# Three causal selects per head group in place of seven, with exponentials stored in another layout and other instruction orders

## The chip, the cores and the metric

The kernel runs on one core of a Trainium2 chip. The metric is the device time of one launch in microseconds. The engines named below are PE (TensorE: matmuls; its weight loads are shown apart as PEld), DVE (VectorE), ACT (ScalarE), POOL (GpSimd) and SP (SyncE, which here issues nearly all DMAs). Every engine has a queue of its own that it works off in order, and engines wait for each other through semaphores.

## The reference, cut to what matters

Two branches read the same 2048 tokens of width 640 and are mixed by a per-token gate g.

Branch A is causal attention inside four segments of 512 tokens, 32 heads of width 20, joined with a memory that is carried from segment to segment:

```
for s in range(4):
    logits = einsum('bhqd,bhkd->bhqk', qs, ks) * scale + mask
    a_dot  = softmax(logits) @ vs
    a_mem  = (phi(qs) @ M) / (phi(qs) @ z + 1e-6)
    o      = g_h * a_mem + (1 - g_h) * a_dot
    M, z   = M + phi(ks).T @ vs, z + sum(phi(ks))
a = o @ wo
out = g * a + (1 - g) * irfft2(rfft2(x) * W)
```

The mask adds -1e9 where the key's position lies behind the query's. Branch B is the filter in the frequency domain in the last line; the kernel does its transforms as matmuls with tables.

## The kernel before

**Staging.** The four segments are worked off in turn. For each one, `project` makes q, k and v, q and k go through a scratch tensor in DRAM into the padded tiles `qkp` (one head per 32 partitions), `attend` does the attention, `mem_update` and `mem_read` the memory. The transforms of branch B (`fft`) run beside segments 0 to 3. `finish_tile` does the last projection with `wo`, adds branch B and stores; for segments 0 to 2 it first needs the reciprocals of the softmax denominators, which go through DRAM: `denominators` loads them (`dnc`), inverts them (`dnr`, L1340), multiplies with a gate (`rc`, L1342), stores them (`r_scr<-rc`) and `finish_tile` loads them again spread over partitions (`r<-r_scr`); then the five steps named `normal` multiply them into `oU` (L1656).

**Attention.** A head group is four heads, so a segment has 8 groups and the kernel 32. Groups are taken in pairs, and a pair has five units (`UNITS`, L580; `qk_unit`, L1356), each of which is a bundle of small matmuls into one and the same block of four PSUM banks, followed by the exponential on ACT from PSUM into the tile `ex` (L1393). Kind 0 (unit a) takes the 512 queries against the first 64-key blocks, kind 1 (unit b) the rest, kind 2 (unit c) what is left of both groups of the pair; the order inside a pair is a, b of the first group, a of the second, c of both, b of the second. Units a and c use weights 64 columns wide, so that two keys' blocks lie beside each other in the array, and unit b uses weights 128 columns wide:

```
    PIECES = (((0, 0, 0, 0, 0, 512), (1, 64, 64, 128, 0, 64), (0, 64, 64, 64, 64, 448)),
              ((1, 0, 0, 192, 0, 320), (2, 0, 0, 320, 320, 192)),
              ((2, 0, 0, 256, 0, 64), (3, 64, 64, 384, 0, 128), (3, 0, 0, 448, 64, 64)))
```

A piece is (128-key block, first key in it, first partition of the result, first query, first column of the result, columns), and each piece is done once for each of the four heads. Segment 3 needs another layout of `ex` for its own way of multiplying with v (`pv_group` instead of `pv_flipped`), so there unit b's exponential is split in two (1280 and 768 elements a partition) and unit c's too (512 each).

**Causal selects.** Whole diagonal blocks are computed, and POOL then sets to zero what lies ahead of the query (`mask`, L1411; the instruction is at L1414). A group has seven selects: two after its exponential a, two after b, three after c; four of them cover 256 elements a partition, two cover 512 elements on 64 partitions, one 512 on 128. The product with v (`pvf` or `pv`) waits for all of them. `ex` has three buffers for the 32 groups.

**The order.** Nothing is placed at run time. `record` lists some 2,300 steps with their dependences, `ORDER` is a list written out by hand or program that says in which order and on which engine each step is issued (an even entry takes a step's first engine, an odd one its second), and `schedule` (L112) only derives the PSUM banks and waits from it. The list `ENDED` is used for one thing: where a step has several waits, `emit` (L254) issues the one first whose step stands later in `ENDED`. Steps made by `either` may go to DVE or POOL, those by `copy_alts` (evacuations of PSUM) to ACT or DVE. On PE the matmuls of one step are issued together; steps have a mode (full array, `qk` tiles of 20 x 64 or 20 x 128, 32-column tiles, 64-column tiles), and neighbours of one mode need no switch of the array.

## Time and profile before

| what | value |
|---|---|
| time, median of 3 runs | 241.98 us (241.62 to 243.56) |
| span of the profiled execution, first to last instruction | 247.9 us (the page gives no other time of it) |
| PE busy | 230.0 us, 93%, 3849 matmuls |
| PEld busy | 139.7 us, 56% |
| DVE busy | 196.3 us, 79% |
| ACT busy | 199.7 us, 81% |
| POOL busy | 165.7 us, 67% |
| selects on POOL (L1414) | 224, together 121.0 us |
| exponentials on ACT (L1393) | 92, together 138.7 us |
| mean granted TensorE clock | 0.972 of full speed |

In the rows of a profile, "out<-in" names the tiles written and read, then follow partitions and elements a partition, the count, the busy time and the mean of one. Numbers behind the last bar are the idle time that the engine had just before these instructions and what ended it. A row of the timeline has the start and the length in microseconds, the engine, the line and the operation; SPq and ACTq are instructions that issue DMAs. Three engines are busy over 79% of the span, so a wait of one of them is mostly filled by the others; the chain of work that ended last tells which one set the end.

### The profile page before, as it was taken

To read this page: it belongs to the slowest core of one execution; us is meant where nothing else is said; L and a number is where in the kernel's file an instruction comes from. 1 tells how busy PE (TensorE), PEld (TensorE's weight loads), DVE (VectorE), ACT (ScalarE), POOL (GpSimd) and SP (SyncE) were. 2 spreads that over 40 slices of the span, in tenths; PEclk is the share of its full clock that TensorE was granted. 3 is DMA by queue.
4 is the path that set the end of the run, shared out by engine and by line. 5 is a ranking of instruction groups with operands and counts; after the bars stand their busy time and mean duration, and the time that the engine had idled before them with its cause. 6 is when DMAs were issued, how large, how long until landed. Compare 5 with 4: busy or idle time off the path is not lost.

```text
span 247.9 us, 9233 instructions
## 1 busy us (share of the span) xinstructions
PE 230.0 (93%) x3849; PEld 139.7 (56%) x3849; DVE 196.3 (79%) x481; ACT 199.7 (81%) x241; POOL 165.7 (67%) x297
## 2 busy tenths in 40 slices
PE   7899999999999999998899999999999975699994
PEld 2574667765465665545566554455444543366794
DVE  0489998799999987888998979979888831755653
ACT  2289688998999989999999899999999864278740
POOL 8532278367969658478939998949898660559640
PEclk9999999999999999999999999999999995599999
DMA  7999979937875864768697543447665977382123
GB/s 174 281 361 206 229 191 230 269 91 203 222 173 163 199 213 114 206 95 252 170 242 208 165 131 99 122 146 192 188 183 128 282 101 81 35 118 81 59 81 109
DMA packets 58924, 42.11 MB, mean 170 GB/s; under 512 B 30020, under 2 KB 55172, under 8 KB 58884
## 3 DMA queue, kind: packets, MB, share of 16 engines
q1 hardware_dynamic: 57844, 40.96, 66.4%
q8 instruction: 30, 0.49, 0.8%
q10 hardware_dynamic: 1040, 0.57, 0.8%
q14 instruction: 10, 0.08, 0.2%
HBM read 23.32 MB, written 12.30 MB: 144 GB/s over the span
## 4 chain that ended last, share of the span: by engine, by line
PE 59%; DVE 15%; DMA 12%; ACT 8%; SPq 3%; issue 2%; DVEq 0%
PE psum L521 52%; PE psum L519 6%; ACT ex L1393 5%; DMA r<-r_scr 3%; DMA r_scr<-rc 3%; DVE Pt L1569 3%; DMA Wt<-in_B_w_i_dram 2%; DMA wk<-in_A_wk_dram 2%; DMA qk_scr<-qu 2%; SPq L553 2%; DVE G L1615 1%; SPq L555 1%; DVE oU L1656 1%; DVE phk L1213 1%; DVE va L1244 1%
## 5 line engine op out<-in xcount | busy, mean ns | idle before, releaser
L1393 ACT ACTIVATE ex<-psum 128x2048 bf16<-128x2048 f32 (+4 forms) x92 | 138.7, 1507 | 13.2 <-PE psum L521 11.4
L1414 POOL TENSOR_SCALAR_AFFINE_SELECT ex<-ex 128x256 bf16<-128x256 bf16 (+2 forms) x224 | 121.0, 562 | 41.2 <-ACT ex L1393 38.3
L521 PE MATMUL psum<-qkp 20*64 20x64 bf16 (+5 forms) x1024 | 31.8, 268 | 4.0 <-ACT ex L1393 2.1
L521 PE MATMUL psum<-xT,wk 128*128 128x256 bf16 (+1 forms) x280 | 33.9, 273 | 0.6 <-DMA wk<-in_A_wk_dram 0.6
L521 PE MATMUL psum<-xT,wq 128*128 128x512 bf16 (+1 forms) x135 | 30.7, 381 | 0.5 <-DMA xT<-in_A_x_dram 0.5
L521 PE MATMUL psum<-wv,xT 128*64 128x320 bf16 (+3 forms) x240 | 30.1, 303 | 0.3 <-DVE va L1244 0.3
L1569 DVE TENSOR_TENSOR Pt<-psum,Wt 128x642 bf16<-128x642 f32 x32 | 25.5, 821 | 2.6 <-PE psum L521 1.5
L521 PEld LDWEIGHTS psum<-qkp 20*64 20x64 bf16 (+1 forms) x1024 | 12.2, 101 | 22.0 <-ACT ex L1393 14.8
L521 PEld LDWEIGHTS psum<-xT,wk 128*128 128x128 bf16 (+1 forms) x280 | 19.9, 97 | 7.1 <-DMA wk<-in_A_wk_dram 1.6
L519 PE MATMUL psum<-wo,oU 128*32 128x320 bf16 x480 | 23.5, 317 | 0.2 <-DVE oU L1664 0.2
L1035 POOL TENSOR_TENSOR xsb<-xf 128x320 bf16<-128x320 bf16 (+2 forms) x12 | 9.5, 788 | 16.2 <-DVE xsb L1035 12.2
L1244 DVE TENSOR_TENSOR va<-psum,ebx 128x320 bf16<-128x320 f32 x32 | 15.2, 483 | 5.0 <-ACT gate L1242 2.9
L521 PEld LDWEIGHTS psum<-wv,xT 128*64 128x64 bf16 (+1 forms) x240 | 14.9, 105 | 7.4 <-issue 2.9
L532 DVE CAST ot<-psum 128x320 bf16<-128x320 f32 x21 | 10.1, 491 | 11.2 <-PE psum L519 8.8
L521 PE MATMUL psum<-big,Cp 128*128 128x321 bf16 (+1 forms) x96 | 18.7, 310 | 0.2 <-DVE G L1615 0.2
L521 PE MATMUL psum<-big,Ac 128*128 128x160 bf16 (+2 forms) x96 | 18.1, 257 | 0.3 <-DVE Pt L1569 0.2
L521 PE MATMUL psum<-ex,va 128*32 128x512 bf16 (+4 forms) x480 | 17.3, 275 | 0.5 <-DVE mem L1289 0.2
L521 PE MATMUL psum<-tt,Yt 128*128 128x256 bf16 (+1 forms) x96 | 16.5, 276 | 1.1 <-DVE Pt L1569 0.4
L1615 DVE TENSOR_TENSOR G<-eo,psum 128x320 bf16<-128x320 f32 x32 | 14.7, 482 | 3.5 <-PE psum L521 2.5
L1201 ACT ACTIVATE et<-qu 128x512 bf16<-128x512 bf16 x25 | 15.6, 629 | 0.2
L519 PEld LDWEIGHTS psum<-wo,oU 128*32 128x32 bf16 x480 | 12.5, 100 | 5.7 <-issue 1.1
L521 PEld LDWEIGHTS psum<-ex,va 128*32 128x32 bf16 x480 | 10.1, 96 | 9.8 <-POOL ex L1414 1.7
(99 smaller groups left out, 393.7 us busy)
## 6 DMA issues: line engine op xcount, KB each, us to landing
qkp<-qk_scr SPq DMA_DIRECT2D x28, 160.0 KB
tt<-tab_tt SPq DMA_DIRECT2D x8, 512.0 KB, 3.8
qk_scr<-qu SPq DMA_DIRECT2D x12, 256.0 KB, 2.4
u_scr<-ub SPq DMA_DIRECT2D x12, 256.0 KB, 4.4
xsb<-in_A_x_dram SPq DMA_DIRECT2D x8, 320.0 KB, 5.9
oU<-u_scr SPq DMA_DIRECT2D x15, 128.0 KB, 4.0
out_dram<-ot SPq DMA_DIRECT2D x12, 160.0 KB
Wt<-in_B_w_r_dram SPq DMA_DIRECT2D x16, 80.2 KB, 3.3
```

The lines of the kernel that those rows point to most:

```text
L519: h = e.matmul(dst, wt, r_, start=st, stop=sp_, **{**kw, "tile_position": (0, q), "skip_group_check": True})
L521: h = e.matmul(o_, l_, r_, start=st, stop=sp_, **kw)
L532: alts["dve"] = (lambda e: e.tensor_copy(dst(), src()), 67 + 1.04 * n, 68.0)
L553: return e.dma_start_transpose(d_, s_)
L555: return e.dma_start(d_, s_)
L1035: self.either(lambda e, dst=dst, src=src, d0=d0, n=n, op=op: e.tensor_tensor(xs.ap(o + dst, [D, 2], [1, n]), xf.ap(src + d0, [321, 2], [1, ...
L1201: self.one("act", lambda e: e.activation(et.ap(0, [1, L]), qsl(), ACT.Exp), L, [qb], [b("et", pi_)], late, name="phi_exp")
L1244: self.one("dve", lambda e: e.tensor_tensor(va.ap(i * H * VW + h0 * VW, [VW, nh], [1, DH]), self.ps(bank, 0, [DH, nh], [1, DH]), self.ebx. ...
L1393: self.one("act", lambda e, d=d, q=q: e.activation(self.ex.ap(*d), self.ps(bank, *q), ACT.Exp, scale=SC), n, [bank], [self.exb(s, 2 * pr + ...
L1414: self.one("pool", lambda e: e.affine_select(self.ex.ap(e0 + d0, [1280, 4], [1, n], np_=np_), self.ex.ap(e0 + s0, [1280, 4], [1, n], np_=np_),
L1569: self.one("dve", lambda e, ri=ri, Pt=Pt, Wt=Wt, wo_=wo_, bank=bank: e.tensor_tensor(Pt.ap(ri * 322, [644, 2], [1, KD]), self.ps(bank, 0, ...
L1615: self.one("dve", lambda e, q=q, n2=n2, bank=bank, eo=eo: e.tensor_tensor(self.G.ap(n2 * D + 639 * q, [1 - 2 * q, 320]), eo.ap(q, [1, 320] ...
```

## The change

- The layout of `ex` is now two blocks of 640 for each head, the same in all four segments: in each, unit a's or b's 512 columns and two strips of 64. The diagonal blocks of a group's four heads then lie at one distance from each other, eight of them.
- `PIECES` gives each unit other pieces: unit b has five pieces with weights 64 columns wide instead of two with 128, unit c four instead of three. The number of columns in each unit stays. A pair has 96 small matmuls in place of 64 (kernel: 1536 in place of 1024).
- Each unit has one exponential in every segment: 80 in place of 92. Unit c writes 64-column strips of both groups with one instruction.
- A group has three selects of 512, 1024 and 1024 elements a partition, on all 128 partitions: 96 in place of 224. The first reads what a and b wrote and writes the strips between; the second finishes these and unit c's strips; the third does the first diagonal blocks. They are recorded behind unit c for the first group of a pair and behind unit b for the second, and no select starts before the group's exponentials a and b are there.
- The product with v reads the new places (`VPIECES`: 512, 128, 256, 256, 128 columns for 512, 384, 192, 64, 128).
- `ENDED` is gone; the order of waits comes from the planner's own end times. `ORDER` is another list for the 2188 steps that are left of 2328.

```diff
-VPIECES = ((0, 0, 512, 0), (1, 512, 384, 128), (2, 896, 192, 320), (2, 1088, 64, 256), (3, 1216, 128, 384))
+VPIECES = ((0, 0, 512, 0), (1, 512, 128, 128), (1, 896, 256, 256), (2, 640, 256, 256), (3, 1152, 128, 384))
...
-              ((1, 0, 0, 192, 0, 320), (2, 0, 0, 320, 320, 192)),
-              ((2, 0, 0, 256, 0, 64), (3, 64, 64, 384, 0, 128), (3, 0, 0, 448, 64, 64)))
+              ((2, 0, 0, 256, 0, 256), (3, 64, 64, 384, 0, 64), (2, 64, 64, 320, 64, 192), (1, 0, 0, 256, 256, 256), (1, 64, 64, 256, 256, 256)),
+              ((1, 0, 0, 192, 0, 64), (1, 64, 64, 192, 0, 64), (3, 0, 0, 448, 256, 64), (3, 64, 64, 448, 256, 64)))
...
+        for i, o in enumerate(sorted(ops, key=lambda o: o.t1)):
+            o.rank = i
...
+        if kind < 2:
+            d, q, n = (e0 + 640 * kind, [1280, 4], [1, 512]), (0, [512, 4], [1, 512]), 2048
         else:
-            outs = [((e0 + sh + n_ * step, [1280, 4], [320, 2], [1, 64]), (n_ * 128, [512, 4], [64, 2], [1, 64])) for n_ in range(2)]
...
+            d, q, n = (e0 + 576, [self.exo(s, g + 1) - e0, 2], [640, 8], [1, 64]), (0, [64, 2], [256, 8], [1, 64]), 1024
+        self.one("act", lambda e: e.activation(self.ex.ap(*d), self.ps(bank, *q), ACT.Exp, scale=SC), n, [bank],
+                 [self.exb(s, 2 * pr + gp, ks) for gp in gps], prio - self.QK_LEAD, name="exp")
+        if u == 3:
+            self.mask(s, 2 * pr, prio)
+        elif u == 4:
+            self.mask(s, 2 * pr + 1, prio)
...
+        def sel(d0, s0, n, base, np_):
+            return lambda e: e.affine_select(self.ex.ap(e0 + d0, [640, 8], [1, n], np_=np_), self.ex.ap(e0 + s0, [640, 8], [1, n], np_=np_),
+                                             [[0, 8], [1, n]], ALU.is_ge, 0.0, base=base, channel_multiplier=-1)
+        x = [self.exb(s, g, k) for k in ("a0", "b0", "c0", "m0")]
+        self.one("pool", sel(512, 0, 64, 64, P), 512, x[:2], x[3:], prio, per=0.793, fix=218, name="mask_first")
+        self.one("pool", sel(512, 512, P, -64, 64), 1024, [], x[2:], prio, per=0.793, fix=218, name="mask_odd")
+        self.one("pool", sel(0, 0, P, 0, P), 1024, [], x[:2], prio, per=0.793, fix=218, name="mask_even")
```

Read against the lists of steps, the two `ORDER` lists have the units of all pairs in one and the same sequence on PE, and the products with v too. They differ in what lies between. Counted in them: switches of PE's mode, 226 before and 212 after. Engines, before and after: outputs evacuated by ACT 11 and 17 of 32 (the others by DVE), products with v evacuated by ACT 8 and 12 of 24, results of the last transform (`eo`) by ACT 10 and 7 of 16, transposes for segment 3 by ACT 4 and 2 of 5, projections by ACT 22 and 21 of 39; foldings of x on POOL 16 and 10 of 51, gate tables on POOL 2 and 4 of 4, `normal` on POOL 2 and 4 of 15. On SP, the load of `wk`'s larger part stood behind the load of an `xsb` part, the transposed loads of x, `beta` and `wk`'s smaller part; now neither `xsb` nor `beta` is ahead of it. For segment 2, eleven DMAs stood between the load of `dnc` and the store of `rc` (five of them `oU` loads just ahead of it); now seven do, in this order: one `qkp`, two `oU`, `gcc`, two `qkp`, one store of outputs. Behind that store come `oU`, `qkp`, a transposed load, `oU`, `g_scr`, `oU`, and then the load of `r`.

More of the change, by code (lines that the diff above doesn't have):

```diff
@@ L110, with schedule @@
             (0, 4): 105.0, (1, 4): 105.0, (2, 4): 105.0, (4, 0): 105.0, (4, 1): 105.0, (4, 2): 105.0}
-    def schedule(self, pools, order, ended, nsem=56):
+    def schedule(self, pools, order, nsem=56):
         ops = self.ops
-        for o in ops:
-            o.rank = len(ops)
-        for i, v in enumerate(ended):
-            ops[v].rank = i
         queue = {e: [] for e in self.eng}
@@ L1361, in qk_unit @@
         gps, kind = unit
-        width = 128 if kind == 2 else 512
         items, rb = [], []
@@ L1381, in qk_unit @@
-        if kind == 0 or (kind == 1 and s < 3):
-            outs = [((e0 + 576 * kind, [1280, 4], [1, 512]), (0, [512, 4], [1, 512]))]
-        elif kind == 1:
-            outs = [((e0 + 576, [1280, 4], [1, 320]), (0, [512, 4], [1, 320])), ((e0 + 960, [1280, 4], [1, 192]), (320, [512, 4], [1, 192]))]
-        elif s < 3:
-            outs = [((e0 + sh, [1280, 4], [step, 2], [1, 128]), (0, [512, 4], [128, 2], [1, 128]))]
-        else:
-            outs = [((e0 + sh + n_ * step, [1280, 4], [320, 2], [1, 64]), (n_ * 128, [512, 4], [64, 2], [1, 64])) for n_ in range(2)]
@@ L1409 @@
-    SH23 = (1088, 896)
-    def mask(self, s, g, np_, d0, s0, n, rk, wk, prio, base, step=64):
-        e0 = self.exo(s, g)
-        self.one("pool", lambda e: e.affine_select(
-            self.ex.ap(e0 + d0, [1280, 4], [1, n], np_=np_), self.ex.ap(e0 + s0, [1280, 4], [1, n], np_=np_),
-            [[0, 4], [step, n // 64], [1, 64]], ALU.is_ge, 0.0, base=base, channel_multiplier=-1), 4 * n, [self.exb(s, g, k) for k in rk],
-            [self.exb(s, g, k) for k in wk], prio, per=0.793, fix=218, name=f"mask{d0}" + "bc"[np_ == P])
+        ks = "abc"[kind] + "0"
```

48 lines of the change are left out of this document (12 added, 36 removed), and 307 rows, old and new, of tables (ENDED, ORDER).

## The prediction

> **What bounds the kernel now.** I first read the page: busy times, chain, costliest groups.
>
> ```profile
> span 247.9 us, 9233 instructions
> PE 230.0 (93%) x3849; PEld 139.7 (56%) x3849; DVE 196.3 (79%) x481; ACT 199.7 (81%) x241; POOL 165.7 (67%) x297
> PE 59%; DVE 15%; DMA 12%; ACT 8%; SPq 3%; issue 2%; DVEq 0%
> L1393 ACT ACTIVATE ex<-psum 128x2048 bf16<-128x2048 f32 (+4 forms) x92 | 138.7, 1507 | 13.2 <-PE psum L521 11.4
> L1414 POOL TENSOR_SCALAR_AFFINE_SELECT ex<-ex 128x256 bf16<-128x256 bf16 (+2 forms) x224 | 121.0, 562 | 41.2 <-ACT ex L1393 38.3
> ```
>
> PE sets the end: 59% of the chain. POOL isn't on it at all, and its selects waited 38.3 us for exponentials. The waits say the same from the other side:
>
> ```profile
> PEld psum L521 <- ACT ex L1393: 14.8, 47, 0.7
> PEld psum L521 <- POOL ex L1414: 1.7, 6, 0.4
> ```
>
> PE's weight loads sat 14.8 us until an exponential had freed the PSUM block, but only 1.7 us, six times, until a select. What a cheaper select can give directly is 1.7 us. The stretches (columns: length, then busy time and count of PE, PEld, DVE, ACT, POOL, clock, DMA) show who could profit:
>
> ```profile
> 100.00:125.00 25.00, 23.49 (x358) 13.22 (x358) 22.93 (x58) 23.97 (x27) 18.53 (x37) 1.00 0.71 181
> 204.00:214.70 10.70, 5.92 (x122) 3.46 (x124) 4.78 (x14) 3.72 (x5) 2.20 (x3) 0.50 0.48 61
> ```
>
> In the middle PE, DVE and ACT are all above 91%, POOL at 74%. Taking work from POOL alone shortens nothing there. From 204 to 214.7 all engines idle, and the clock is at half: a hole, whose cause is read below.
>
> **The change part by part.** *Selects.* The groups by shape:
>
> ```profile
> L1414 POOL TENSOR_SCALAR_AFFINE_SELECT ex<-ex 128x256 bf16<-128x256 bf16 x128 | 59.5, 476 | 38.7 <-ACT ex L1393 37.4
> L1414 POOL TENSOR_SCALAR_AFFINE_SELECT ex<-ex 64x512 bf16<-64x512 bf16 x64 | 42.6, 670 | 1.8 <-ACT ex L1393 0.9
> L1414 POOL TENSOR_SCALAR_AFFINE_SELECT ex<-ex 128x512 bf16<-128x512 bf16 x32 | 22.0, 690 | 0.6
> ```
>
> From 256 to 512 elements a select grows by 214 ns, so 262 ns are fixed. A 1024 select isn't in the trace: the line gives 690 + 2 x 214 = 1118 ns; it may cost up to two of 512, 1380 ns. A group paid 4 x 476 + 2 x 670 + 690 = 3934 ns and will pay 690 + 2 x 1118 = 2926 (at most 3450). Over 32 groups POOL loses 32 us (at least 15) and falls to about 133 us. Hidden behind ACT and PE as shown, I cost it at 0 to -1.7 us and take 0, since the same wait can come back, next.
>
> *The wait that is added.* Selects used to start after exponential a; now a group's first needs a and b. For a group that ends with b, the time from its last exponential to v was 670 + 476 = 1146 ns and becomes 2926; for one that ends with c, 476 + 476 + 690 or so = 1.6 us becomes 2 x 1118 = 2.2. Behind the waiting select on POOL stand the other selects, W additions (L1574) and `normal`; PE's next matmuls stand behind v. What covers it is PE work between a group's last unit and its v: counted in the order lists, at least 10 steps before (median 26.5) and at least 16 after (28.5). A step takes 230.0 / 1073 = 0.214 us on average. A group that ends with b needs 0.33 + 1.88 + 2.93 = 5.1 us, 24 steps; 5 of 32 groups have fewer than they need. Added up, they are short by 1.5 us, and 3 groups before by 1.7: the new list moved v back as far as it had to. I take 0.
>
> *Exponentials.* Segments 0 to 2 keep theirs. In segment 3 the rows are
>
> ```profile
> L1393 ACT ACTIVATE ex<-psum 128x2048 bf16<-128x2048 f32 x56 | 105.2, 1879 | 7.9 <-PE psum L521 6.7
> L1393 ACT ACTIVATE ex<-psum 128x1024 bf16<-128x1024 f32 x12 | 12.3, 1023 | 1.1 <-PE psum L521 0.8
> L1393 ACT ACTIVATE ex<-psum 128x1280 bf16<-128x1280 f32 x8 | 9.9, 1239 | 3.0 <-PE psum L521 3.0
> L1393 ACT ACTIVATE ex<-psum 128x768 bf16<-128x768 f32 x8 | 6.5, 810 | 0.3
> L1393 ACT ACTIVATE ex<-psum 128x512 bf16<-128x512 f32 x8 | 4.8, 598 | 1.1 <-PE psum L521 1.0
> ```
>
> Unit b pays 1239 + 810 - 1879 = 170 ns less, eight times; unit c 2 x 598 - 1023 = 173 less, four times: -2.05 us of ACT. The new list gives ACT more evacuations (6 of outputs, 4 of products with v, less 3 `eo`, 2 transposes, 1 projection), some 2.5 us at 0.44 to 0.6 each, so ACT stays at 200 us. Bounds 0 to -2.05; the end of segment 3 lies in the hole, so I take a quarter, -0.5. Unit c's strips of 64 might stream slower; no row shows it, nearest is the 1024 form: 0.
>
> *Matmuls.* 512 more, columns unchanged. The PE timeline has each kind with its follower:
>
> ```profile
> 100.61 0.40 PE L521 MATMUL psum<-qkp 20*128 20x320 bf16 x8
> 100.94 0.63 PE L521 MATMUL psum<-tt,Yt 128*65 128x256 bf16 x4
> ...
> 103.71 0.32 PE L521 MATMUL psum<-qkp 20*64 20x64 bf16 x24
> 103.96 1.25 PE L521 MATMUL psum<-xT,wq 128*128 128x512 bf16 x5
> 105.05 0.38 PE L521 MATMUL psum<-tt,Yt 128*65 128x256 bf16 x2
> 105.36 0.43 PE L521 MATMUL psum<-qkp 20*64 20x512 bf16 x12
> 105.72 0.39 PE L521 MATMUL psum<-xT,wq 128*128 128x512 bf16 x1
> ```
>
> Unit b with 8 matmuls holds PE 0.33 us, c with 24 0.25, a with 12 0.36: PE follows columns (512, 256, 512), hardly the count. The new b (20, weights as in a) should take between its 0.33 and a's 0.36: 32 x 0.015 = +0.5 us; c with 32 stays or gains 8 x 4 ns: 16 x 0.015 = +0.2. Together +0.6, bounds 0 to +5.3 (c's 250 / 24 = 10.4 ns for each of 512).
>
> The Trainium skill, TensorEngine Tiling, Instruction Overhead, says that each matmul has an overhead of about 60 cycles and that one column takes as long as 60. By it, in a row, 512 x 25 ns = 12.8 us would be added, an estimate from that page; the 24 matmuls in 0.25 us, 10 ns each, speak against it for tiles that work side by side.
>
> *Mode switches.* Five 512-column matmuls take 105.05 - 103.96 = 1.09 us, 0.218 each; unit a with the same columns 0.36, so entering and leaving cost 0.14, or 0.07 a switch. 226 - 212 = 14 fewer: -1.0 us (0 to -2.0).
>
> *DVE beside longer selects.* One group shows what a select does to DVE, first with its mean, then with its minimum/median/maximum in ns:
>
> ```profile
> L1213 DVE TENSOR_SCALAR phq<-qu 128x512 bf16<-128x512 bf16 x15 | 5.3, 363 | 0.0
> L1213 DVE TENSOR_SCALAR phq<-qu x15: 273/283/712, 34.7 to 157.4; 128x512 bf16<-128x512 bf16 x15
> ```
>
> The slowest is 429 ns above the median, about one 256 select: it seems to be held until POOL's instruction is over. If so, the mean hold goes with the squares of the selects' lengths: 128 x 0.476² + 64 x 0.67² + 32 x 0.69² = 73 before, 32 x (0.69² + 2 x 1.118²) = 95 after, 1.3 times. The mean is 80 ns above the median; some 130 of DVE's instructions read bf16 from SBUF alone as this one does, so they may be held 10 us now and 13 later, an estimate. I take 15% of these 3 us, DVE's share of the chain: +0.4, bounds 0 to +3.
>
> *Start.* The chain at the start:
>
> ```profile
> 0.78 0.41 SPq L555
> 1.25 1.21 SPq L553
> 2.51 0.57 SPq L555
> ...
> 6.33 5.36 DMA wk<-in_A_wk_dram
> ```
>
> The first and third are `xsb` and `beta`, now behind `wk`: -0.98 us if the landing stays 5.36 us, 0 if bandwidth sets it. `beta` comes later, and v's first evacuation needs it; that is microseconds away. I take -1.0.
>
> *The hole.* The timeline from 187 us:
>
> ```profile
> 187.12 0.51 SPq L555 DMA_DIRECT2D dnc<-u_scr  x1
> 192.65 0.47 DVE L1342 TENSOR_TENSOR rc<-dnr,gcc 128x128 bf16<-128x128 f32 x1
> 192.69 3.18 SPq L555 DMA_DIRECT2D oU<-u_scr  x5
> 195.92 0.60 SPq L555 DMA_DIRECT2D r_scr<-rc  x1
> 202.69 0.56 SPq L555 DMA_DIRECT2D r<-r_scr  x1
> 209.78 1.77 DVE L1656 TENSOR_TENSOR oU<-oU,r 128x512 bf16<-128x512 bf16 x5 [7.79 <-DMA r<-r_scr]
> 212.50 0.46 PE L521 MATMUL psum<-G,fbg 128*32 128x320 bf16 x4 [4.58 <-DVE on L1455]
> ```
>
> `rc` is ready at 193.1, but five `oU` loads are being issued, so its store goes at 195.9, lands late, and DVE stands 7.79 us in front of five `normal`, with segment 3's work queued behind; PE idles 4.58 us. In the new list those five loads stand elsewhere, but the load of `gcc` comes after `dnc`: 187.6 + 0.3 (`qkp`) + 1.2 (two `oU`) + 0.6 = 189.7, plus the landing
>
> ```profile
> DMA to landing us min/median/max: 4.6/4.6/4.6
> ```
>
> gives 194.3 and a store at about 194.6 instead of 195.9: -1.3 us. Five `normal` still stand in front of segment 3's work. Bounds 0 and -4.6; whether runs without the profiler have the hole at this size isn't shown.
>
> Fewer waits and their other order: nothing visible, 0. The rest of the new list (evacuations moved, six foldings to DVE) I cost at 0; DVE and ACT keep their loads within 4 us.
>
> Sum: -0.5 + 0.6 - 1.0 + 0.4 - 1.0 - 1.3 = -2.8 us. The page gives no time of the profiled execution but its span, 247.9, 5.9 above the median of 241.98; the difference is taken from the median: **239.2 us**.
>
> **The rivals.** *No change:* the small terms drown, middle stretches stay bound by PE, ACT and DVE, and the hole stays. For: ACT keeps 200 us. 241 to 243. That selects of 1024 cost more than the line says ends here too.
>
> *The hole closes:* all of PE's 4.58 us goes instead of 1.3, so -6.1 in all, and a little more if the clock doesn't fall to 0.50: 235.5. For: five DMA issues fewer ahead of the store. Against: a transposed load stands ahead of `r`'s load.
>
> *Slower: v waits for selects.* The place is PE in front of v; the price hangs on how long the steps between are. At 0.214 us a step it is nothing; at 0.15 us, the shortages from the lists add up to 15.4 us after and 9.5 before, +6; then, with half of the gains left, 246.5. It decides from about 0.18 us on (+2.3). For: products with v now wait 1.8 us longer behind b; against: the median distance grew.
>
> *Slower: matmuls cost by the piece,* +5.3 us by c's row, 244.5 with the gains.
>
> **How the numbers follow.** Forecast, 237 to 241: 0.42. Hole closes: 0.18. No change: 0.15. v waits: 0.20. Matmuls by the piece: 0.05. A measurement of this kernel tells about 1% (2.4 us) from none, so the forecast's own 0.42 falls on both sides of 239.6: 0.30 and 0.12. Faster by over 1%: 0.18 + 0.30 = 0.48; within 1%: 0.15 + 0.12 = 0.27; slower: 0.25. The range takes in all five cases and some 1.5 to 2.5 us beyond for what the moved steps of the new list may do: 233 to 248.
>
> **What would show it.** Right: POOL near 133 us with 1024 selects near 1.12 us; unit b near 0.35 us on PE; ACT near 200; `wk` landed near 10.7; the store of `rc` under 7.5 us after `dnc`. Wrong: PE's waits for `ex` from POOL well above 1.7 us, or a hole later and longer than 4.6 us.

## The result and the profile after

The changed kernel takes 256.99 us (median of 4 runs, 255.57 to 259.32) where the kernel before takes 241.8 beside it on the same chip: 1.063 times as long, 95% interval 1.056 to 1.070. The prediction was 239.2 with a range of 233 to 248. The change costs 15 us, and the prediction was wrong in its sign. Some executions fall into a slower state of the chip, so every time below is the median of the runs outside it, while brackets behind a time give all runs.

The page of the changed kernel, its first lines and its chain by engine:

```profile
span 254.3 us, 10109 instructions
PE 225.9 (89%) x4347; PEld 143.0 (56%) x4361; DVE 210.1 (83%) x478; ACT 199.8 (79%) x234; POOL 138.0 (54%) x167
PE 44%; DVE 28%; ACT 10%; issue 5%; DMA 5%; SPq 5%; POOL 1%; POOLq 0%; DVEq 0%
```

POOL fell from 165.7 to 138.0 us, as it was meant to, and has 1% of the chain. But DVE, which has three instructions fewer than before, works 13.8 us longer, and its share of the chain went from 15% to 28%. PE has lost the 15% that DVE and ACT gained. These shares differ between executions, too: the profile of the kernel before with only its waits' order changed, which takes the same time (below), has PE 50% and DVE 20%. The busy times are the firmer sign.

The groups by shape of the changed kernel, selects first:

```profile
L1264 POOL TENSOR_SCALAR_AFFINE_SELECT ex<-ex 128x1024 bf16<-128x1024 bf16 x32 | 35.6, 1112 | 0.8
L1264 POOL TENSOR_SCALAR_AFFINE_SELECT ex<-ex 64x1024 bf16<-64x1024 bf16 x32 | 35.2, 1104 | 12.0 <-ACT ex L1252 11.4
L1264 POOL TENSOR_SCALAR_AFFINE_SELECT ex<-ex 128x512 bf16<-128x512 bf16 x32 | 21.7, 680 | 40.0 <-ACT ex L1252 39.0 <-ACT gate L1112 1.0
```

The selects are as long as forecast and together 92.5 us, not 121.0. (The second of a group works on 64 partitions, not on all 128 as the list of changes has it, and takes as long as the third.) Nor do the matmuls wait much more for them, 2.7 us against 2.0 before (the waits):

```profile
PEld psum L519 <- ACT ex L1252: 16.3, 51, 0.7
PEld psum L519 <- POOL ex L1264: 2.5, 7, 0.6
PE psum L519 <- POOL ex L1264: 0.2, 1, 0.2
```

So the loss is not the wait that replaces a wait. It shows in the stretches (length, then busy time and count of PE, PEld, DVE, ACT, POOL, clock, DMA share, GB/s). First two of the kernel before, then the same two of the changed one:

```profile
50.00:75.00 25.00, 24.31 (x349) 13.77 (x348) 24.14 (x63) 23.09 (x28) 19.42 (x37) 1.00 0.68 168
150.00:175.00 25.00, 23.66 (x348) 13.31 (x349) 23.14 (x58) 23.38 (x28) 18.84 (x35) 1.00 0.54 148
```

```profile
50.00:75.00 25.00, 21.29 (x332) 13.04 (x331) 23.11 (x50) 20.25 (x27) 12.99 (x20) 0.93 0.73 180
150.00:175.00 25.00, 21.36 (x295) 11.89 (x296) 22.13 (x36) 19.80 (x22) 14.42 (x21) 0.93 0.41 112
```

DVE is nearly as busy as before (22 to 23 us of 25 against 23 to 24), but gets 50 instructions done instead of 63, and 36 instead of 58. PE and ACT lose 2 to 4 us in both stretches, which are among those that lose most. DVE's instructions have become longer. Which ones, the groups say; before, then after:

```profile
L1214 DVE TENSOR_TENSOR phk<-phk,et 128x512 bf16<-128x512 bf16 x15 | 7.2, 490 | 0.0
L1213 DVE TENSOR_SCALAR phq<-qu 128x512 bf16<-128x512 bf16 x15 | 5.3, 363 | 0.0
L1574 DVE TENSOR_TENSOR Yt<-Pt 128x321 bf16<-128x321 bf16 x16 | 5.7, 380 | 0.0
L1656 DVE TENSOR_TENSOR oU<-oU,r 128x512 bf16<-128x512 bf16 x13 | 6.0, 501 | 7.8 <-DMA r<-r_scr 7.8
```

```profile
L1084 DVE TENSOR_TENSOR phk<-phk,et 128x512 bf16<-128x512 bf16 x15 | 11.6, 776 | 0.0
L1083 DVE TENSOR_SCALAR phq<-qu 128x512 bf16<-128x512 bf16 x15 | 7.5, 509 | 0.0
L1424 DVE TENSOR_TENSOR Yt<-Pt 128x321 bf16<-128x321 bf16 x16 | 8.7, 554 | 0.1
L1506 DVE TENSOR_TENSOR oU<-oU,r 128x512 bf16<-128x512 bf16 x11 | 8.1, 769 | 0.0
```

Same shapes, same work for each instruction, means 40 to 58% longer. All four read and write bf16 in SBUF alone. Instructions of DVE that read PSUM show nothing of the kind: `Pt<-psum,Wt` has a mean of 821 ns before and 819 after, and of its 32 instructions, 27 of which began beside a busy POOL before and 14 after, none lasted over 0.83 us. The timeline of the changed kernel shows why at its worst place (DVE's row, then POOL's, from two views):

```profile
231.00 3.53 DVE L1514 TENSOR_TENSOR oU<-oU,mT 128x640 bf16<-128x640 bf16 x1
```

```profile
229.79 5.68 POOL L1264 TENSOR_SCALAR_AFFINE_SELECT ex<-ex 128x1024 bf16<-128x1024 bf16 x6
```

An addition that takes 0.48 us elsewhere (the median of its group) takes 3.53 us here: it begins inside a row of six selects that leaves no gap, and it ends 0.94 us before that row does. From the single starts and ends in the trace: 0.92 us of the select it met were left, three more followed, and only during the sixth did it get through. That sixth select took 1.33 us instead of 1.08. A second place, again DVE and then POOL:

```profile
103.56 2.62 DVE L1084 TENSOR_TENSOR phk<-phk,et 128x512 bf16<-128x512 bf16 x1
```

```profile
101.67 2.85 POOL L1264 TENSOR_SCALAR_AFFINE_SELECT ex<-ex 128x512 bf16<-128x512 bf16 x3 [1.28 <-ACT ex L1252]
104.50 1.40 POOL L1424 TENSOR_TENSOR Yt<-Pt 128x321 bf16<-128x321 bf16 x2
```

Here 0.42 us of work took 2.62 us, held by the last of three selects and then by two additions of POOL as well.

What this does to PE can be read in the two stretches above (PE's row after its longest wait in each, and DVE's row ahead of the second):

```profile
65.97 0.51 PE L519 MATMUL psum<-Mz,phq 128*128 128x154 bf16 x3 [2.31 <-DVE ub L530]
151.62 2.35 DVE L1212 TENSOR_TENSOR rc<-dnr,gcc 128x128 bf16<-128x128 f32 x1
154.86 0.63 PE L519 MATMUL psum<-xT,wq 128*128 128x512 bf16 x1 [2.70 <-DVE va L1114]
```

In the first, four selects in a row keep POOL busy from 60.42 to 65.13 us, three instructions of DVE in succession (`Yt`, `phk`, `Yt`) take 1.21, 1.30 and 1.21 us, and the evacuation `ub` behind them in DVE's queue comes late. In the second, `rc`, 0.29 us of work, takes 2.35 us, and `Bt` and `va` stand behind it. PE's clock is halved for 3.4 us from the last half microsecond of either wait on, which is the 0.93 of these stretches; so the clock did not cause these waits.

To count the delays of DVE I took, for each DVE instruction that reads and writes bf16 in SBUF alone (137 before, 139 after), what it lasted above the lower quartile of its own group (line, tiles and shape), and call it its **hold**. The holds add up to 9.2 us before (longest 0.56) and 23.8 us after (longest 3.05): +14.6, where DVE's busy time rose by 13.8. (`rc`, which reads f32 in SBUF, isn't in this count: its three instructions took 1.0 us before and 3.8 after.) 46 of these instructions met a busy POOL before and 45 after, so it is not that more are hit: each hit costs 0.53 us instead of 0.20. 41 of the 45 have one form (to 0.07 us; 45 of 46 before): the hold is what was left of POOL's instruction, less 0.13 us. The other four did not get in where one POOL instruction followed on another, and are together 5.8 us above this form. They are four of 20 hits that had another POOL instruction right behind; before it was none of 23 (and 1 of 25 in the kernel before with only its waits' order changed, below).

The Trainium skill, SBUF — State Buffer, Who interferes with whom, has the mechanism: DVE's second pair of SBUF ports is GpSimd's only one, and for DVE instructions that use it (a two-port mode, or two inputs in SBUF) whichever of the two engines begins first has the pair for its whole instruction, while the other is blocked. The trace agrees as far as the rest of one instruction goes, and in the other direction too: the 21 selects of the changed kernel that began during such a DVE instruction are 0.08 to 0.14 us longer in the mean than the rest of their shape. That the wait can run on through the next instructions, the page does not say, and the experiments below test it.

### The profile page after: what moved, and what is told of

It reads as the page before. It is cut to its first block, busy times and chain, and to the rows that moved or that the text cites. A ratio compares the mean times of both kernels' runs of the same rounds, so it can differ in the third digit from the quotient of the medians.

```text
span 254.3 us, 10109 instructions
## 1 busy us (share of the span) xinstructions
PE 225.9 (89%) x4347; PEld 143.0 (56%) x4361; DVE 210.1 (83%) x478; ACT 199.8 (79%) x234; POOL 138.0 (54%) x167
## 4 chain that ended last, share of the span: by engine, by line
PE 44%; DVE 28%; ACT 10%; issue 5%; DMA 5%; SPq 5%; POOL 1%; POOLq 0%; DVEq 0%
PE psum L519 39%; ACT ex L1252 8%; PE psum L517 5%; DVE Pt L1419 4%; SPq L553 3%; DMA xsb<-in_A_x_dram 3%; DMA qk_scr<-qu 2%; DVE Yt L1424 2%; DVE phk L1084 2%; DVE qu L530 2%; DVE G L1465 2%; SPq L551 2%; DVE oU L1514 1%; DVE phq L1083 1%; DVE Cp L530 1%
## 5 line engine op out<-in xcount | busy, mean ns | idle before, releaser
L1252 ACT ACTIVATE ex<-psum 128x2048 bf16<-128x2048 f32 (+1 forms) x80 | 136.5, 1707 | 18.4 <-PE psum L519 16.8
L1264 POOL TENSOR_SCALAR_AFFINE_SELECT ex<-ex 64x1024 bf16<-64x1024 bf16 (+2 forms) x96 | 91.1, 965 | 52.8 <-ACT ex L1252 50.4
L519 PE MATMUL psum<-qkp 20*64 20x64 bf16 (+4 forms) x1536 | 33.0, 255 | 4.4 <-ACT ex L1252 2.1
L519 PE MATMUL psum<-xT,wq 128*128 128x512 bf16 (+1 forms) x121 | 27.4, 392 | 5.2 <-DVE va L1114 2.7
L519 PEld LDWEIGHTS psum<-qkp 20*64 20x64 bf16 x1536 | 14.6, 104 | 24.6 <-ACT ex L1252 16.3
L905 POOL TENSOR_TENSOR xsb<-xf 128x318 bf16<-128x318 bf16 (+1 forms) x7 | 5.8, 832 | 27.3 <-DVE xsb L905 27.3
L517 PE MATMUL psum<-wo,oU 128*32 128x320 bf16 x480 | 20.0, 299 | 0.2 <-DVE oU L1514 0.2
L519 PE MATMUL psum<-ex,va 128*32 128x256 bf16 (+2 forms) x480 | 17.4, 275 | 3.0 <-DVE Bt L530 1.5
L519 PE MATMUL psum<-big,Cp 128*128 128x321 bf16 (+1 forms) x96 | 17.2, 302 | 0.9 <-DVE G L1465 0.9
L519 PEld LDWEIGHTS psum<-xT,wq 128*128 128x128 bf16 (+1 forms) x135 | 9.9, 99 | 12.9 <-DVE Bt L530 2.6
L1424 POOL TENSOR_TENSOR Yt<-Pt 128x321 bf16<-128x321 bf16 x16 | 11.9, 753 | 6.9 <-PE psum L519 6.7
```

The costliest lines, as they stand in the source:

```text
L517: h = e.matmul(dst, wt, r_, start=st, stop=sp_, **{**kw, "tile_position": (0, q), "skip_group_check": True})
L519: h = e.matmul(o_, l_, r_, start=st, stop=sp_, **kw)
L905: self.either(lambda e, dst=dst, src=src, d0=d0, n=n, op=op: e.tensor_tensor(xs.ap(o + dst, [D, 2], [1, n]), xf.ap(src + d0, [321, 2], [1, ...
L1252: self.one("act", lambda e: e.activation(self.ex.ap(*d), self.ps(bank, *q), ACT.Exp, scale=SC), n, [bank], [self.exb(s, 2 * pr + gp, ks) f ...
L1264: return lambda e: e.affine_select(self.ex.ap(e0 + d0, [640, 8], [1, n], np_=np_), self.ex.ap(e0 + s0, [640, 8], [1, n], np_=np_), [[0, 8] ...
L1424: fn = lambda e, r=r, a0=a0, a1=a1, op=op, Pt=Pt, Yt=Yt: e.tensor_tensor(Yt.ap(r * 322, [1, KD]), Pt.ap(a0 * 322, [1, KD]), Pt.ap(a1 * 322 ...
```

## The experiments

The theories at the outset: **P**, the long selects keep DVE from its port; **O**, the new order list loses by itself; **M**, the matmuls in more pieces lose. All times stand beside runs of the kernel before on the same chip, at 242.0 to 242.4 us.

**Layout and order exchanged.** First the new layout and its three selects in the order list of before:

```diff
-        23, 0, 90, 24, 76, 104, 74, 2, 28, 4, 6, 8, 10, 26, 12, 14, 72, 16, 30, 18, 20, 34, 46, 48, 36, 44, 202, 42, 190, 178, 214, 180, 204, 182,
...
+        46, 0, 90, 26, 74, 23, 2, 4, 36, 24, 6, 8, 28, 10, 12, 72, 14, 16, 30, 18, 20, 178, 64, 34,
...
```

> The layout, the exponentials, the pieces and the three selects of the changed kernel, with the order list of the kernel before: its 224 selects are taken out, a group's first new select stands where its last select for a and b stood, the other two where its last select of all stood. Theory P (the long selects hold DVE's shared port; the changed profile has 24.2 us of hold on DVE against 9.3): 250 to 255 us, with DVE's held instructions (L1084, L1506, L1424) as slow as in the changed kernel. Theory O (the new list itself loses, by its start and its waits): 241 to 245 us. Theory M (the 512 more matmuls cost 2.5 ns each as the units show, 1.3 us in all): adds 1 us to either.

Measured 264.17 us (261.23 to 264.85), ratio 1.085 (1.075 to 1.095). The waits:

```profile
PEld psum L519 <- POOL ex L1265: 16.0, 15, 2.0
PE psum L519 <- POOL ex L1265: 11.3, 13, 1.7
```

With the old order the products with v do wait for the selects, 27.3 us counted on PE and PEld against 2.7 in the changed kernel. The new list removes this wait; with the old list the change costs 22 us.

Then the reverse, layout, exponentials and seven selects of before in the new list:

```diff
-VPIECES = ((0, 0, 512, 0), (1, 512, 128, 128), (1, 896, 256, 256), (2, 640, 256, 256), (3, 1152, 128, 384))
+VPIECES = ((0, 0, 512, 0), (1, 512, 384, 128), (2, 896, 192, 320), (2, 1088, 64, 256), (3, 1216, 128, 384))
...
-        if u == 3:
-            self.mask(s, 2 * pr, prio)
...
+            if ks == "a":
+                self.mask(s, g, P, 512, 0, 64, ("a0",), ("m1",), prio, 64)
...
```

> The kernel before with its own layout, pieces and seven selects, but issued by the new order list: a group's seven stand where the three stand (two, two and three), the second exponentials of segment 3 right behind the first ones, and waits ordered by the planner's end times. Theory P: 242 to 247 us, since the selects are short again. Theory O: 253 to 258 us, since the list is the one of the changed kernel.

Measured 262.35 us (261.55 to 265.98), ratio 1.082 (1.074 to 1.090), with 15.6 and 9.2 us of PE's waits on selects. Both runs lie outside what either P or O gave. Each list fits only its own selects, so these two runs cannot give the list's own share of the time: they add a wait that neither kernel has.

They do tell something of the holds. By the same count these are some 16 us with the long selects in the old list and some 22 us with the short selects in the new one, where they stand in rows of two or three; DVE is busy for 204.4 and 206.3 us, against 196.3 before and 210.1 after. The selects of the second kernel have the shapes of the kernel before, and yet 9 of 33 of its instructions that could be held through a next one were, the longest 1.90 us. So the length of the selects is not the only thing that makes holds: the new list makes them too, at least in a kernel that waits like this one.

**Only the waits' order.** The kernel before without `ENDED`, the waits of a step ordered by the end times that the planner computes:

```diff
-        for i, v in enumerate(ended):
-            ops[v].rank = i
...
+        for i, o in enumerate(sorted(ops, key=lambda o: o.t1)):
+            o.rank = i
```

> The kernel before with nothing changed but the order in which a step's several waits are issued, by the planner's own end times as in the changed kernel. All theories: 241 to 243 us, no change; if not, the waits' order is a part of the loss.

242.5 us, ratio 1.003 (0.999 to 1.007): no part of the loss.

**The long selects cut in two.** The changed kernel with two selects of 512 for each of 1024, at the same places:

```diff
...
+                for k in range(0, 8, m):
+                    h = e.affine_select(self.ex.ap(e0 + 640 * k + d0, [640, m], [1, n], np_=np_), self.ex.ap(e0 + 640 * k + s0, [640, m], [1, n], np_=np_),
+                                        [[0, m], [1, n]], ALU.is_ge, 0.0, base=base, channel_multiplier=-1)
+                return h
+            m = 8 if n == 64 else 4
...
```

> The changed kernel with each select of 1024 elements cut into two of 512 at the same place of the order: POOL works 32 x 524 = 17 us more, but no instruction holds longer than 0.69 us. Theory P: 249 to 253 us and DVE's hold down to some 15 us. Theory O: 257 us, or a little more by POOL's extra work.

250.15 us (249.89 to 252.19), ratio 1.032 (1.025 to 1.038): 6.8 us less than the changed kernel, although POOL has more to do. From its page:

```profile
PE 227.1 (91%) x4347; PEld 143.5 (57%) x4361; DVE 201.1 (80%) x478; ACT 199.3 (80%) x234; POOL 148.2 (59%) x231
```

POOL +10.2 us, DVE -9.0, time -6.8. Shorter instructions on an engine off the chain, with more work in all, make the kernel faster: this speaks for P against O and M, which both stay as they were here.

**The long selects nearly away.** Two of the three selects in the changed kernel, five of the seven in the kernel before, cut to 16 elements, so that most of the zeroing is left out; the edit of the changed one:

```diff
...
+            k, w = (8, n) if n == 64 else (1, 16)
+            return lambda e: e.affine_select(self.ex.ap(e0 + d0, [640, k], [1, w], np_=np_), self.ex.ap(e0 + s0, [640, k], [1, w], np_=np_),
+                                             [[0, k], [1, w]], ALU.is_ge, 0.0, base=base, channel_multiplier=-1)
```

> The changed kernel with its second and third select cut to 16 elements each (most of the causal zeroing is left out), all at the same place of the order with the same waits. Theory P: 244 to 248 us, the hold on DVE under 5 us. Theory O: 254 to 257 us.

> The kernel before with five of a group's seven selects cut to 16 elements (most of the causal zeroing is left out), all at the same place. With the same in the changed kernel at 244.8 us, this tells what the selects cost in the kernel before. Theory P: 237 to 240 us, since 9 us of hold on DVE go; then the changed kernel without its selects is still 5 to 7 us slower, and that part is the new list and the small matmuls. If it stays at 241 to 242 us, selects cost the kernel before nothing and some 3 us of the loss are list and matmuls.

The changed kernel falls to 244.54 us (ratio 1.007, 1.002 to 1.012) with DVE at 192.7, the kernel before to 240.5 (0.995, 0.992 to 0.999). So these selects cost the changed kernel 12.4 us (13.5 by the ratios) and the kernel before 1.2 to 1.6. A difference of 4.0 us (2.9 by the ratios) is left that has nothing to do with long selects.

**Six selects of at most 512, old order.** The new layout with its selects cut so that each can stand where a select of before stood:

```diff
...
+    def mask(self, s, g, k, prio):
+        self.sel(s, g, k, 512, 0, 64, 64, P, ("ab"[k] + "0",), (f"m{k}",), prio, f"mask_strip{k}")
+        self.sel(s, g, k, 0, 0, P, 0, P, (), ("ab"[k] + "0",), prio, f"mask_diag{k}")
+    def odd(self, s, g, prio):
+        for k in range(2):
+            self.sel(s, g, k, 512, 512, P, -64, 64, (), ("c0", f"m{k}"), prio, f"mask_odd{k}")
```

> The changed kernel's layout, exponentials and matmuls, but six selects a group, none over 512 elements a partition, two behind each of exponentials a and b and two behind c, issued by the order list of the kernel before at the places where the seven stood. Theory P (a select costs by its length, through DVE's shared port, and by how late it may start; nothing else in the change costs much): 241 to 244 us, PE's wait for selects under 5 us, unit b 0.362 us on PE as in the changed kernel. Theory M (layout and smaller matmul pieces carry the loss): 248 us or more.

254.6 us, ratio 1.051 (1.045 to 1.056): over 10 us above what was expected. Its waits:

```profile
PEld psum L519 <- POOL ex L1267: 8.8, 10, 1.4
PE psum L519 <- POOL ex L1267: 6.4, 9, 1.1
```

PE's waits on selects are 15.2 us against 2.0 before, and DVE stands at 201.1, 4.8 above before. The holds are some 13 us by the same count. So the wait and the hold are both there, and the run doesn't separate them. That the old list leaves too little room behind the later selects of a group is argued from these waits, not shown by itself.

**Pieces of 256.** By P as I then had it (a DVE instruction is held for the rest of the one select it meets), still shorter selects should hold less (the line shown is against the halves):

```diff
...
-            m = 8 if n == 64 else 4
+            m = 4 if n == 64 else 2
...
```

> The changed kernel with its selects cut into pieces of 256 elements a partition, ten a group at the same three places. POOL works 1.8 us more a group than in the changed kernel. Theory P has two terms here: the hold falls below that of halves (10.4 us) but a group's zeroing ends later by 1.8 us: 250 to 256 us, with PE waiting for selects over 5 us. If only the hold counted: 247 to 249 us.

264.25 us (263.99 to 268.05), ratio 1.095 (1.089 to 1.100), missed upward. PE's waits on selects are 21.3 us, which was expected to grow, but DVE got worse too instead of better (its page, and then one group's minimum, median and maximum in ns):

```profile
PE 234.8 (88%) x4361; PEld 145.5 (55%) x4361; DVE 213.9 (80%) x478; ACT 200.0 (75%) x234; POOL 168.7 (63%) x391
```

```profile
L1084 DVE TENSOR_TENSOR phk<-phk,et x15: 410/421/2776, 25.7 to 120.1; 128x512 bf16<-128x512 bf16 x15
```

The group's median is that of undisturbed work, the maximum is 2.36 us above it, while a select in this kernel takes 0.42 us in the mean. Up to ten selects stand one behind the other here, most of them starting some 40 ns before the one before ends. The instruction with that maximum was held for the rest of one select, four more and an addition of POOL; another, at 248.24 us, got in only behind eight selects, where POOL's row had a gap. The holds add up to 28.5 us; of 41 instructions that met a select with another POOL instruction right behind, 14 were held through it. My theory of the single instruction fell with this run. In its place: **R**, a DVE instruction that finds POOL at work is held until POOL's row of instructions has a gap; against **S**, it is the one instruction after all, and the long holds are chance.

**A gap between POOL's instructions.** Each POOL instruction waits until POOL's own one before it is complete, in the changed kernel, in the two with cut selects (there a semaphore of its own does the same between the pieces), and in the kernel before:

```diff
-            o.need_inc = o.dma
+            o.need_inc = o.dma or o.eng == "pool"
...
+            if e == "pool" and count[e]:
+                self.eng[e].wait_ge(prog[e], count[e])
```

> The changed kernel, with every instruction of POOL waiting for POOL's own one before it to be complete. In the traces so far a POOL instruction that isn't waiting for another engine starts some 40 ns before the one before it ends, so a row of them leaves no gap. Theory R (a DVE instruction that finds POOL at work is held until POOL's row of instructions has a gap, not only until the one instruction is over): the longest hold falls from 3.05 us to 1.2 at most, the holds together from 23.8 us to 14 to 18, DVE's busy time from 210.1 to 201 to 206. Theory S (held until the one instruction is over; the 3.05 us was a chance of two or three in succession): holds 21 to 27 us in all, DVE 207 to 213. POOL itself has some 0.1 us more between its 167 instructions, up to 17 us of its 110 idle ones, so the time is the weaker witness: by R 249 to 255, by S 256 to 261.

> The kernel with the 1024-element selects cut in two, with the same gap between all POOL instructions, the halves too. R: longest hold from 1.79 us to 0.8 at most, holds together from 17.2 us to 8 to 12, DVE from 201.1 to 193 to 197, time 244 to 249 (from 250.15). S: holds 15 to 19, DVE 199 to 203, time 250 to 254.

> The kernel with the selects in pieces of 256 elements (ten a head group), with the gap between all POOL instructions. The two theories are furthest apart here. R: longest hold from 2.87 us to 0.6 at most, holds together from 28.5 us to 5 to 10, DVE from 213.9 to 191 to 197. S: holds 25 to 31, DVE 210 to 217. POOL is lengthened by 320 gaps of some 0.1 us, 32 us, and PE's waits for selects (9.8 us without the gaps) can grow by as much as R gives back: time by R 250 to 268, by S 268 to 285.

> The kernel before with the same gap between all POOL instructions. Control for the gap: if the gap itself makes the kernel faster, by something other than the holds, it does so here too. In before no DVE instruction was held longer than 0.56 us, that is not through a second instruction of POOL, and the holds are 9.2 us in all. Theory R: little to gain (holds 7 to 9.5 us, DVE 194 to 197) and some 20 us more of gaps on POOL, which is 68 per cent busy: 241.5 to 246. If the gap helps by something of its own: 234 to 239, as it took 6 us off the changed kernel.

In the traces the median distance between two POOL instructions goes from -26 to +130 ns in the changed kernel, and to some 70 to 80 in the two with cut selects. What came of it (the holds by my count from the traces; waits are PE's and PEld's on selects):

| kernel | holds without the gap, with | longest | DVE busy | waits | time, us |
|---|---|---|---|---|---|
| changed | 23.8, 15.0 | 3.05, 0.92 | 210.1, 198.9 | 2.7, 5.1 | 256.99, 249.76 |
| 1024 cut in two | 17.2, 14.4 | 1.79, 0.77 | 201.1, 199.7 | 5.5, 19.3 | 250.15, 254.19 |
| pieces of 256 | 28.5, 9.1 | 2.87, 0.77 | 213.9, 194.9 | 21.3, 49.3 | 264.25, 292.15 |
| before | 9.2, 12.1 | 0.56, 0.70 | 196.3, 201.2 | 2.0, 14.5 | 241.8, 256.94 |

Two of the pages with gaps, of the changed kernel and of the pieces of 256:

```profile
PE 227.3 (91%) x4347; PEld 143.6 (57%) x4361; DVE 198.9 (80%) x478; ACT 199.5 (80%) x234; POOL 140.7 (56%) x167
```

```profile
PE 241.8 (83%) x4347; PEld 151.5 (52%) x4361; DVE 194.9 (67%) x478; ACT 200.4 (69%) x234; POOL 184.4 (63%) x391
```

R's sharpest case came out: with pieces of 256 the holds fall to a third and DVE loses 19 us, though POOL now works 15.7 us longer. In the changed kernel the holds fall to 15.0, inside the 14 to 18 that R gave, the longest to 0.92, and the time by 7.2 us to 249.76 (248.63 to 253.55; ratio 1.027, 1.021 to 1.033). In no kernel with gaps is a DVE instruction held through a second one of POOL. Several of R's numbers were missed. In the changed kernel DVE falls further than R had it (201 to 206). With the halves the holds are 14.4 where 8 to 12 were expected, and DVE's 199.7 lies where S had it, so there only the longest hold speaks for R. In pieces of 256 the longest is 0.77, not under 0.6; these longest ones lie beside POOL's other instructions (`fbg`, `oU`) of 1.2 to 1.4 us, which a gap doesn't shorten. The times of these two kernels, 254.19 and 292.15, are above what R gave, and above what S gave too. And R as I put it is too strong: without gaps most DVE instructions did get in at the next boundary (16 of 20 in the changed kernel). What holds is that without a gap it can lose again there, and with one it never did.

The control says that a gap is no gain of itself: the kernel before loses 14.6 us with it (ratio 1.060, 1.055 to 1.064), far more than the 241.5 to 246 that I had given, and its holds grow from 9.2 to 12.1 us, since 65 instructions in place of 46 meet a busy POOL. A gap turned out at 0.13 us instead of the 0.1 I had reckoned with, and instructions that followed directly overlapped by 0.036 before, so each pays 0.166. In the kernel before, 198 of 296 followed directly, which makes some 33 us of POOL, an estimate; PE's waits for selects show it:

```profile
PEld psum L523 <- POOL ex L1416: 7.4, 12, 1.4
PE psum L523 <- POOL ex L1416: 6.8, 13, 1.4
```

The same price shows in the halves and the pieces of 256, where PE's waits for selects grow to 19.3 and 49.3 us. So the gap shows the mechanism by DVE's rows, and in these four kernels it paid only in the changed one, where POOL has the fewest instructions.

**What is left with short selects.** List and layout exchanged once more, with the selects cut to 16 elements, since PE then waits far less for them (3.5 and 3.9 us, against 27.3 and 24.8 above); first new layout in the old list, then old layout in the new list:

```diff
...
+            k, w = (8, n) if n == 64 else (1, 16)
...
```

```diff
...
+        keep = d0 != s0 and np_ == P
+        k, j, w = (4, n // 64, 64) if keep else (1, 1, 16)
...
```

> The new layout, exponentials, matmul pieces and three selects in the order list of before, with the second and third select cut to 16 elements, so that most of the zeroing is left out. With short selects the changed kernel still stood 4.1 us over the kernel before with short selects (244.77 against 240.67). List (the new order list loses them): this one comes out near 241 (240 to 242.5). Matmuls (the new layout's pieces, 512 more matmuls, lose them): 244 to 247.

> The layout, exponentials, matmul pieces and seven selects of before in the new order list, five of the seven selects cut to 16 elements, so that most of the zeroing is left out. List: 244 to 247. Matmuls: near 241 (240 to 242.5).

The new layout in the old list: 246.99 us (245.19 to 248.31), ratio 1.017 (1.011 to 1.023). By the expectation this is the matmuls. Its trace says otherwise: both kernels issue the 80 bundles of `qk` matmuls in one sequence, and up to the 68th, at 194 us, each starts within 1.1 us of its place in the kernel before; the loss comes behind that, in segment 3. Against the kernel before with short selects it is at most 1.6 us. So that is, in this one execution, a bound for the new layout with its additional matmuls up to there. The old layout in the new list has only two runs that count, 242.15 and 244.27 us (all twelve: 242.15 to 248.84), one inside what the matmuls' case gave and one inside the list's. Both mixtures also wait more for selects than the unmixed kernels with short selects (1.1 us in the changed one, 0.2 in the one before). So the 3 to 4 us that are left aren't divided between list and layout.

## Why the prediction was wrong

**"DVE beside longer selects" is the step that failed.** It was the right mechanism with the right direction, and was sized at +0.4 us, bounds 0 to +3. Without the long selects the changed kernel gains 12.4 us and the kernel before 1.2 to 1.6, so the term measured some 11 us, and PE's wait for selects is only 0.7 us of it. Three things were wrong in it. The holds were put at 10 us, growing to 13; they were 9.2 and became 23.8. The factor 1.3 came from the squares of the selects' lengths; but a hold is what is left of a select less 0.13 us, and the squares of the lengths less 0.135 grow by 2.19 / 1.345 = 1.63 a group, not 1.3, which makes 15. Some 5.8 us more are the holds that ran on through the next POOL instructions, which no row of before showed: with a longest hold of 0.56 us, it could be read as "until POOL's instruction is over" and nothing more. Some 3 us are left over. Nor did the prediction ask what the new list does to the holds, and the short selects in that list alone bring them to some 22 us. And of the added holds 15% were taken as time, DVE's share of the chain. That share doesn't say what longer DVE instructions cost: the run with short selects gives back 12.4 us of time for 17.4 us of DVE's (210.1 against 192.7), some 70%.

**Selects at 0.** POOL at 138 against 133 and selects of 1.11 us against 1.12 were right. That work saved on POOL "shortens nothing" was right as well. What was missed is that POOL's work has a price on DVE whether or not PE waits for POOL. Of the signs that were to show the prediction right, POOL's time, the select's 1.11 us, unit b, ACT and the store of `rc` all came out near their numbers; none of them looks at DVE.

**"The wait that is added."** The counting of steps in the lists was right: PE's waits on selects went from 2.0 to 2.7 us. The rival *v waits for selects* did not happen in the changed kernel; in the old list it would have, with 27.3 us. With the matmuls below, both rivals that were to make the kernel slower are out, and it is slower in a way that was no rival but a small term.

**Exponentials.** ACT stands at 199.8, as forecast.

**Matmuls.** Unit b, from its start to the next matmul, and unit c, two rows each of the changed kernel's PE timeline:

```profile
84.12 0.43 PE L519 MATMUL psum<-qkp 20*64 20x256 bf16 x20
84.49 0.24 PE L519 MATMUL psum<-big,Ac 128*128 128x160 bf16 x1
...
97.27 0.33 PE L519 MATMUL psum<-qkp 20*64 20x64 bf16 x32
97.53 1.55 PE L519 MATMUL psum<-wv,xT 128*64 128x320 bf16 x20
```

0.37 and 0.26 us; over all units the medians are 0.362 (0.330 before) and 0.2625 (0.25), 32 x 0.0325 + 16 x 0.0125 = +1.2 us instead of +0.6. The rival *by the piece* (+5.3) is out, and so is the estimate of 12.8 us, which set in a row the overhead of some 60 cycles that the Trainium skill, TensorEngine Tiling (Array Packing), Instruction Overhead, gives each matmul: 32 matmuls in 0.26 us are 8 ns each.

**Start.** The first three units start 2.0 to 2.8 us earlier, twice the -1.0 forecast, and the fourth 4.1 us later. The loads that were moved back are what the early chain now runs through (SP's rows of the changed kernel, then a piece of its chain):

```profile
6.99 0.43 SPq L553 DMA_DIRECT2D beta<-in_A_beta_dram  x1
7.47 0.71 SPq L553 DMA_DIRECT2D xsb<-in_A_x_dram  x1
```

```profile
7.47 7.54 DMA xsb<-in_A_x_dram
```

"Microseconds away" was said of `beta`; the chain runs through `xsb`, for which no cost of coming later was taken. With short selects the fourth unit is 4.0 us late too, so this is in the list and not in the selects. There it fades to 0.6 us by the eighth unit.

**The hole.** The store of `rc` goes 207.3 - 200.5 = 6.8 us after the load of `dnc`, under the 7.5 forecast (8.8 before), and PE has no such stall there any more:

```profile
L553 SPq DMA_DIRECT2D dnc<-u_scr x3: 519/556/606, 112.6 to 200.5; - x3
L553 SPq DMA_DIRECT2D r_scr<-rc x3: 344/348/479, 169.0 to 207.3; - x3
```

But there was little to win: the profiled execution of before, with its span of 247.9, was a late one. Of 67 runs of that kernel beside the experiments 66 have spans of 238.9 to 244.7 us, and one 247.8. With only the waits' order changed, and a time that didn't differ, the page has

```profile
span 241.6 us, 9233 instructions
```

and 6 to 8 us less at the units behind the hole; DVE stands 0.72 us for `r` there, not 7.79. That is also why the two profiled spans differ by 6.4 us and the timed runs by 15. I had read a term of -1.3, and a rival of 0.18, from a stall that most executions don't have at this size.

Of the mode switches (-1.0) nothing can be told from these runs. By the accounts that can be made, the 15.2 us are 12 to 13 of selects in the changed kernel less 1 to 2 in the one before, and 3 to 4 of the new list and layout, not divided. The prediction had put the rest of the new list at 0.

## What to carry to other kernels

When VectorE and GpSimd both work in SBUF, an instruction on GpSimd has a second price beside its own time: the wait of each VectorE instruction that meets it. Fewer and longer GpSimd instructions can lower GpSimd's total and still cost time, and so can an order that puts them in rows. Before merging or moving them, count how many VectorE instructions of the kind that waited here (those that read and write bf16 in SBUF alone, and `rc`) run beside them, and weigh what is left of a longer instruction and rows without a gap, not the total. And look for it in the means of groups whose shape has not changed: 490 to 776 ns for the same instruction is most of the case in one row.

## What the runs showed of the hardware

Three things I had not expected. First, a held VectorE instruction doesn't always get in where GpSimd's instruction ends: 4 of 20 such cases in the changed kernel, 5 of 28 with the selects in halves and 14 of 41 with pieces of 256 were held through the next instruction or several, up to 3.05 us; with a distance of about 0.07 to 0.13 us between GpSimd's instructions, none was. It is rarer under the old list: none of 23 cases in the kernel before, but 1 of 25 (1.91 us) with only its waits' order changed, 1 of 22 with the long selects and 2 of 33 with six selects; under the new list it was 9 of 33 even with the selects of before, though none of 12 with short ones. What in the list does it, with instructions that follow each other as closely in both, stays open. Second, cutting long selects into halves won 6.8 us and into quarters lost 7.3, so of three lengths the middle one was the best; with the quarters PE's waits for selects grew as well. Third, making GpSimd wait for its own last instruction costs some 0.166 us where two would follow directly, since they otherwise overlap by 0.036 us.
